# One chunk in one of eight widths for the last 512 rows of the second feed-forward, with a short last block packed

## The chip, the cores and the metric

The kernel runs on one core of one Trainium2 chip. The metric is the device time of one execution in microseconds. Each kernel is timed in several runs, and the median is quoted. The profile is of one further execution.

## The reference

Three stages follow one another, on float32 data (the last stage's weights come as float64).

```python
x = attention(q, k, v)                     # 1536 rows of 512
logits = x @ w_gate                        # 8 experts
expert_idx = np.argmax(logits, axis=1)
for i in range(N):                         # capacity 384 rows for each expert
    e = expert_idx[i]
    if counts[e] < capacity:
        disp[e, counts[e]] = x[i]; counts[e] += 1; keep[i] = True
y = relu(disp @ w1) @ w2                   # for each expert
out[i] = gate_w[i] * y[...] if keep[i] else 0
h = out @ w_in                             # 512 -> 2048
g = relu(h) ** 2
return g @ w_out                           # 2048 -> 512
```

A row that its expert has no room for is zero after the second stage, and so is its row of the result: relu of zero, squared, times `w_out`. The inputs are drawn from one fixed seed. The reference's own routing of them fills the experts with 290, 123, 98, 163, 117, 165, 92 and 488 rows; clipped at 384 each, 1432 rows are kept.

## The kernel before

The expert stage writes its results to a DRAM buffer `yd`, with expert after expert packed without gaps (`off` holds where each starts, `dst` each row's place, L787 to L793). Kept rows are therefore rows 0 to 1431 of `yd`; the rest stay as they were filled, with zeros and a token number that is out of bounds. Each row of `yd` carries its token's number in a last column.

The second feed-forward (L1022 to L1105) works in that packed order. Its 1536 rows are cut into four chunks, 512, 512, 256 and 256 (`chunks`, L949). A chunk has 16 steps `f`, one for each 128 of the 2048 hidden units. All products are made of float32 numbers split into a high and a low part of fp32r, three products (high by high, high by low, low by high) for each:

- `stage_a` (L1038, matmuls L1049): 12 matmuls, 4 parts of the depth by 3 products, each with the chunk's rows as moving columns (512 or 256), into the tile `a`; then ScalarE's relu into `xb` (L1051) and VectorE's square (L1052).
- `stage_g` (L1055): ScalarE rounds the squares to the high part `gh` (L1060), VectorE subtracts for the low part `gl` (L1061).
- `stage_b` (L1064, matmuls L1073): for each block `t` of 128 rows, 3 matmuls with 128 rows of `gh` or `gl` as weights and 512 columns of `w_out` moving. They add up in PSUM over the 16 steps, in one tile `out` for each block. After step 15, `out` is copied to a `raw` tile, by VectorE for even `t` (L1080) and ScalarE for odd `t` (L1078), and GpSimd issues an indirect DMA that scatters the 128 rows to their tokens (L1081). Rows whose token number is out of bounds are not written.

The order of work is written out by hand: `stage_a` of step i, `stage_g` of step i, `stage_b` of step i-1. TensorE runs this order without reordering. A scatter is declared free of a conflict with the one issued just before it, not with the one two before; so each scatter waits until the second last has landed.

The rows of the next chunk are loaded and transposed during the chunk before (`load_y`, L951; transposes L968, four for each block of 128 rows), at steps 7, 9, 11 and 13.

Run-time branches exist already. Ahead of the expert stage every engine reads the eight counts and `head` (the row at which the last expert starts) from the tile `cnt` into registers (L989, L991, written by VectorE at L788 to L790). `more` (L926) runs a further block of 128 rows for an expert only if its count asks for it, and L1018 loads the first chunk again if `head` is below 512.

Of the kernel before, what the change touches and what calls it, by code (L numbers as in the profile page):

```python
# [8 lines left out]
F32 = mybir.dt.float32  # L9
F32R = mybir.dt.float32r  # L10
BF16 = mybir.dt.bfloat16
I32 = mybir.dt.int32
# [4 lines left out]
P = 128  # L17
# [16 lines left out]
def kernel(  # L34
# [15 lines left out]
    nc = tc.nc  # L50
    B, H, S, D = q.shape
    NTOK, DM = out.shape
    E = w_gate.shape[1]
# [5 lines left out]
    NFF = FF // P  # L59
# [6 lines left out]
    nblk = (cap + P - 1) // P  # L66
# [10 lines left out]
    const = ctx.enter_context(tc.tile_pool(name="const", bufs=1))  # L77
# [7 lines left out]
    banks = dict(s=[0, 1], pt=[2], ot=[3], bg=[4, 5, 6], lg=[7])  # L85

    def ps(tag, name):
        banks[tag].append(banks[tag].pop(0))
        return psum.tile([P, 512], F32, tag=f"b{banks[tag][-1]}", name=name)
# [7 lines left out]
    stream, held, eager, slot = [], 0, False, 0  # L97
# [193 lines left out]
    tok = const.tile([P, NQB], I32, name="tok")  # L291
# [29 lines left out]
    if fast:  # L321
# [22 lines left out]
        for g in range(3 if stack else 1):  # L344
            x = own[g * HS : (g + 1) * HS]
            nc.gpsimd.affine_select(x, x, pattern=[[-NS, H], [0, D]], compare_op=ALU.is_ge, fill=0.0, base=0, channel_multiplier=1)
            nc.gpsimd.affine_select(x, x, pattern=[[NS, H], [0, D]], compare_op=ALU.is_ge, fill=0.0, base=NS - 1, channel_multiplier=-1)
    else:
        for j in range(NJ):
            m = ap_.tile([P, S], F32, name=f"m{j}")  # L350
# [366 lines left out]
    for u in range(len(units) + PL + 1):  # L717
# [4 lines left out]
        if u < len(units):  # L722
            n, c = units[u]
# [17 lines left out]
        m, c = divmod(u, HP)  # L741
# [30 lines left out]
    if nblk:  # L772
        src = xrp.tile([P, nblk, E], I32, name="src")
        nc.vector.tensor_scalar(src.rearrange("p b e -> p (b e)"), inv, float(NOBODY), None, op0=ALU.add)
        free = const.tile([P, nblk, E], F32, name="free")
        nc.vector.tensor_scalar(
            free.rearrange("p b e -> p (b e)"), inv, 0.0, float(NOBODY), op0=ALU.is_ge, op1=ALU.mult
        )
        p_ = ps("lg", "cnt")
        nc.tensor.matmul(p_[:, :E], ones, runoh, start=True, stop=True)  # L780
        cntf = const.tile([P, E], F32, name="cntf")
        nc.vector.tensor_scalar(cntf, p_[:, :E], float(cap), None, op0=ALU.min)

        off = const.tile([P, E], F32, name="off")
        nc.vector.memset(off[:, 0:1], 0.0)
        for e in range(1, E):
            nc.vector.tensor_add(off[:, e : e + 1], off[:, e - 1 : e], cntf[:, e - 1 : e])  # L787
        cnt = const.tile([P, E + 1], I32, name="cnt")  # L788
        nc.vector.tensor_copy(cnt[:, :E], cntf)
        nc.vector.tensor_copy(cnt[:, E:], off[:, E - 1 :])  # L790
        dst = const.tile([P, nblk, E], I32, name="dst")
        nc.vector.tensor_add(free, free, spot.unsqueeze(2).to_broadcast([P, nblk, E]))
        nc.vector.tensor_add(dst, free, off.unsqueeze(1).to_broadcast([P, nblk, E]))  # L793
    att.__exit__(None, None, None)
    banks = dict(s=[0, 1, 2], iv=[3], pt=[4], ot=[5], bg=[6, 7])
# [15 lines left out]
    def x_at(e, b):  # L811
        return xring[min(b, XB - 1), e % 2]

    def gate_at(e, b):
        return gate[2 + b % 2 if b else e % 2]
# [9 lines left out]
    def pre(e, b):  # L825
        if e >= E or b >= nblk:
            return
        p_ = ps("bg", "xT")
        for c in range(KD):
            nc.tensor.transpose(p_[:, c * P : (c + 1) * P], x_at(e, b)[:, c * P : (c + 1) * P], ident)  # L830
        xT[e, b] = xTs[min(b, 1)]
        h_, l_ = (x.rearrange("p c n -> p (c n)") for x in xT[e, b])
        nc.scalar.copy(h_, p_)
        nc.vector.tensor_sub(l_, p_, h_.bitcast(F32))
        g_ = gate_at(e, b)
        nc.vector.tensor_scalar(g_, x_at(e, b)[:, DM:], 1e-9, None, op0=ALU.add)
        nc.vector.reciprocal(g_, g_)
# [108 lines left out]


    CH = 512
    chunks = [(c0, CH) for c0 in range(0, NTOK - CH, CH)] + [(NTOK - CH, CH // 2), (NTOK - CH // 2, CH // 2)]  # L949
    NCH = len(chunks)  # L950
    x2T = {0: tuple(x2p.tile([P, KD, CH], F32R, name="x2A" + x) for x in "hl")}  # L951
    last = (E - 1) % 2
# [2 lines left out]
    def load_y(c, tags):  # L955

        c0, w = chunks[c]

        def ld(t):
            if t < w // P:  # L960
                r0 = c0 + t * P
                nc.sync.dma_start(yts[t % len(yts)], yd[r0 : r0 + P, :])

        def go(t):
            yt = yts[t % len(yts)]
            p_ = ps(tags[t % 2], "x2T")
            for kk in range(KD):
                nc.tensor.transpose(p_[:, kk * P : (kk + 1) * P], yt[:, kk * P : (kk + 1) * P], ident)  # L968
            n = c0 // P + t
            nc.gpsimd.tensor_copy(tok[:, n : n + 1], yt.bitcast(I32)[:, DM:])  # L970
            pv = p_.rearrange("p (k n) -> p k n", k=KD)
            hv, lv = (x[:, :, t * P : (t + 1) * P] for x in x2T[c])
            nc.scalar.copy(hv, pv)
            nc.vector.tensor_sub(lv, pv, hv.bitcast(F32))
            ld(t + len(yts))

        for t in range(len(yts)):
            ld(t)
        return [lambda t=t: go(t) for t in range(w // P)]
# [9 lines left out]
        vals = [nc.values_load(cnt[0:1, e : e + 1], min_val=0, max_val=cap) for e in range(E)]  # L989
    if nblk:  # L990
        head = nc.values_load(cnt[0:1, E : E + 1], min_val=0, max_val=NTOK)  # L991
    pre(0, 0)
    its = []
    for e in range(E):
        g = e + 1
# [28 lines left out]
    ffp = ctx.enter_context(tc.tile_pool(name="ffp", bufs=1, side="right"))  # L1024
    WO.alloc()
    x2T[1] = tuple(ffp.tile([P, KD, CH], F32R, name="x2B" + x) for x in "hl")
    for c in range(2, NCH - 1):
        x2T[c] = x2T[c % 2]
    x2T[NCH - 1] = tuple(x[:, :, CH // 2 :] for x in x2T[NCH - 2])
    zf = zb.bitcast(F32)  # L1030
    zw = zf.shape[1]
    for t in range(NQB):
# [3 lines left out]
    outp, gT, its, scattered = {}, {}, [], []  # L1036

    def stage_a(c, f):  # L1038
        nonlocal its
        if f == 0:  # L1040
            its = load_y(c + 1, ("pt", "ot")) if c + 1 < NCH else []
        a_ = ps("bg", "a")
        xh, xl = x2T[c]
        w = chunks[c][1]
        for kk in range(KD):
            r = slice(f % 2 * 512 + kk * P, f % 2 * 512 + kk * P + P)
            wh, wl = WI.h[f // 2][:, r], WI.l[f // 2][:, r]
            for m, (a, bb) in enumerate(((wh, xh), (wh, xl), (wl, xh))):
                nc.tensor.matmul(a_[:, :w], a, bb[:, kk, :w], start=(kk == 0 and m == 0), stop=(kk == KD - 1 and m == 2))  # L1049
        r_ = xring[f % 2, last][:, :w]  # L1050
        nc.scalar.activation(r_, a_[:, :w], AF.Relu)  # L1051
        nc.vector.tensor_mul(r_, r_, r_)  # L1052
        gT[c, f] = r_

    def stage_g(c, f):  # L1055
        r_ = gT[c, f]
        gh = ffp.tile([P, CH], F32R, tag="gh", name="gh", bufs=2)
        gl = ffp.tile([P, CH], F32R, tag="gl", name="gl", bufs=2)
        gh, gl = (x[:, : chunks[c][1]] for x in (gh, gl))
        nc.scalar.copy(gh, r_)  # L1060
        nc.vector.tensor_sub(gl, r_, gh.bitcast(F32))  # L1061
        gT[c, f] = (gh, gl)

    def stage_b(c, f):  # L1064
        gh, gl = gT.pop((c, f))
        if f == 0:
            outp[c] = [ps("s" if t < 3 else "iv", "out") for t in range(chunks[c][1] // P)]
        wh, wl = WO.h[f // 2], WO.l[f // 2]
        r = slice((f % 2) * 512, (f % 2) * 512 + 512)
        for t in range(chunks[c][1] // P):  # L1070
            cs = slice(t * P, (t + 1) * P)
            for m, (a, bb) in enumerate(((gh, wh), (gh, wl), (gl, wh))):
                nc.tensor.matmul(outp[c][t], a[:, cs], bb[:, r], start=(f == 0 and m == 0), stop=(f == NFF - 1 and m == 2))  # L1073
            if f == NFF - 1:
                n = chunks[c][0] // P + t
                o_ = raw_tile()[:, :DM]
                if t % 2:
                    nc.scalar.copy(o_, outp[c][t])  # L1078
                else:
                    nc.vector.tensor_copy(o_, outp[c][t])  # L1080
                i = nc.gpsimd.indirect_dma_start(  # L1081
                    out=out, out_offset=bass.IndirectOffsetOnAxis(ap=tok[:, n : n + 1], axis=0), in_=o_, in_offset=None,
                    bounds_check=NTOK - 1, oob_is_err=False,
                )

                if scattered:
                    tc.declare_no_dep(i.ins, scattered[-1].ins, reason="rows of different tokens")
                scattered.append(i)

    steps = [(c, f) for c in range(NCH) for f in range(NFF)]  # L1090
    def tick():
        if not ticks.done():
            ticks.tick()

    for i in range(len(steps) + 1):
        if i < len(steps):
            c, f = steps[i]
            turn = f >= 7 and f % 2 and its
            stage_a(c, f)
            tick()  # L1100
            stage_g(c, f)
            if turn:
                its.pop(0)()
        if i >= 1:
            stage_b(*steps[i - 1])  # L1105


# [27 lines left out]
```

## Time and profile before

| | us |
|---|---|
| median of 3 runs | 624.29 |
| lowest and highest of them | 622.31, 625.81 |
| the profiled execution's own time | 622.56 |
| span of the profiled execution | 620.8 |
| first matmul of the second feed-forward, from the span's start | 333.15 |
| its third chunk (rows 1024 to 1279) begins on TensorE | 518.60 |
| its last `stage_b` begins on TensorE | 611.14 |
| last scatter is issued | 614.89 |

Times in the rows count from the span's start. The profiled execution's own time is 1.76 us above its span. PE is TensorE's matmul unit, PEld its weight load, DVE VectorE, ACT ScalarE, POOL GpSimd, SP the queue that issues plain DMAs; a `q` behind a name is that engine's sequencer, which runs ahead of the engine. Matmuls are pipelined: the duration of one row overlaps the next matmul's, so rates are read from start to start.

### The profile page before, as it was taken

Reading aid. Unit: us, or ns where it says so; the run is one execution under the profiler, and the core shown is the slowest. Engines: PE = TensorE matmul, PEld = TensorE weight load, DVE = VectorE, ACT = ScalarE, POOL = GpSimd, SP = SyncE. Lnnn points to the kernel's source line nnn. Section 1 sums busy time; section 2 is a strip of 40 time slices with the busy share of each in tenths; the row PEclk is TensorE's granted clock in tenths of the full one; section 3 lists DMA queues with packets and bytes.
Section 4 is the critical chain, followed back from the end, with each engine's and each line's share of the span. In section 5 each row is a group of like instructions: output and inputs, shape, how many; then the busy total and the mean of one; then the engine's idle time right before and its main releaser. Section 6 shows DMA issues by size and latency. Waiting matters only on the chain. (4 is left out here: it accounts for less than half of the span.)

```text
span 620.8 us, 9781 instructions
## 1 busy us (share of the span) xinstructions
PE 588.8 (95%) x3437; PEld 470.4 (76%) x3439; DVE 359.6 (58%) x847; ACT 305.1 (49%) x681; POOL 136.3 (22%) x235
## 2 busy tenths in 40 slices
PE   7999999979999999998798999999999999999994
PEld 4778777738887777776676777888888888998983
DVE  3788888647259967948544899983222323333331
ACT  4888878626247847646423456553212222323221
POOL 8444544342134413431010000000200001101001
PEclk9999999979999999999899899999999999999998
DMA  8697994456337966857482555610100000000000
GB/s 183 160 224 153 236 184 127 141 141 205 126 108 269 341 205 200 314 172 248 142 304 70 190 167 202 199 39 0 69 1 17 18 0 35 35 1 35 1 1 20
DMA packets 74664, 81.99 MB, mean 132 GB/s; under 512 B 42248, under 2 KB 53512, under 8 KB 74608
## 3 DMA queue, kind: packets, MB, share of 16 engines
q1 hardware_dynamic: 70608, 72.45, 40.3%
q0 software_dynamic: 4000, 8.82, 4.1%
q8 instruction: 32, 0.52, 0.3%
q14 instruction: 24, 0.20, 0.1%
HBM read 69.29 MB, written 16.27 MB: 138 GB/s over the span
## 5 line engine op out<-in xcount | busy, mean ns | idle before, releaser
L1051 ACT ACTIVATE xb<-a 128x512 f32<-128x512 f32 (+1 forms) x64 | 31.5, 492 | 151.6 <-PE a L1049 151.6
L1052 DVE TENSOR_TENSOR xb<-xb 128x512 f32<-128x512 f32 (+1 forms) x64 | 35.8, 559 | 116.8 <-ACT xb L1051 116.8
L1073 PE MATMUL out<-yh,gl 128*128 128x512 f32 x192 | 76.8, 400 | 2.4 <-DVE gl L1061 2.1
L1073 PE MATMUL out<-yh,gh 128*128 128x512 f32 x192 | 77.4, 403 | 0.5 <-ACT gh L1060 0.5
L1073 PE MATMUL out<-yl,gh 128*128 128x512 f32 x192 | 76.5, 399 | 0.0
L1049 PE MATMUL a<-x2Ah,xh 128*128 128x256 f32 (+1 forms) x192 | 61.5, 320 | 0.3 <-PEq L1018 0.3
L1049 PE MATMUL a<-x2Al,xh 128*128 128x256 f32 (+1 forms) x192 | 61.3, 320 | 0.2 <-DVEq L1018 0.2
L1049 PE MATMUL a<-x2Ah,xl 128*128 128x256 f32 (+1 forms) x192 | 61.1, 318 | 0.0
L1081 POOL DMA_INDIRECT out_dram<-raw,tok x12 | 12.0, 998 | 215.4 <-DVE raw L1080 168.9
L451 ACT ACTIVATE p<-p,nm 128x260 f32<-128x260 f32 (+2 forms) x96 | 46.8, 489 | 17.1 <-DVE nm L439 16.0
L1061 DVE TENSOR_TENSOR gl<-xb,gh 128x512 fp32r<-128x512 f32 (+1 forms) x64 | 35.6, 557 | 27.5 <-PE out L1073 14.4
L916 POOL DMA_INDIRECT yd<-ys,dst x14 | 25.5, 1819 | 116.2 <-POOLq L926 50.5
L1060 ACT CAST gh<-xb 128x512 fp32r<-128x512 f32 (+1 forms) x64 | 32.9, 514 | 29.4 <-DVE xb L1052 29.4
L1073 PEld LDWEIGHTS out<-yh,gl 128*128 128x128 f32 x192 | 36.5, 190 | 13.4 <-DVE gl L1061 4.4
L146 DVE TENSOR_TENSOR yl<-raw,yh 128x512 fp32r<-128x512 f32 x64 | 40.4, 685 | 6.2 <-ACT yh L145 6.2
L1073 PEld LDWEIGHTS out<-yh,gh 128*128 128x128 f32 x192 | 36.3, 189 | 7.9 <-ACT gh L1060 1.4
L1073 PEld LDWEIGHTS out<-yl,gh 128*128 128x128 f32 x192 | 36.5, 190 | 7.2
L1049 PEld LDWEIGHTS a<-x2Ah,xh 128*128 128x128 f32 x192 | 36.1, 188 | 5.0 <-issue 0.7
L1049 PEld LDWEIGHTS a<-x2Al,xh 128*128 128x128 f32 x192 | 36.1, 188 | 4.7 <-DVEq L1018 0.5
L1049 PEld LDWEIGHTS a<-x2Ah,xl 128*128 128x128 f32 x192 | 36.4, 189 | 2.9
L145 ACT CAST xh<-raw 128x512 fp32r<-128x512 f32 x64 | 36.3, 619 | 1.2 <-DMA raw<-in_moe_w_dram 0.9
L145 ACT CAST yh<-raw 128x512 fp32r<-128x512 f32 x64 | 35.5, 624 | 2.6 <-PEq L926 1.7
(199 smaller groups left out, 1398.6 us busy)
## 6 DMA issues: line engine op xcount, KB each, us to landing
raw<-in_moe_w_dram SPq DMA_DIRECT2D x64, 512.0 KB, 5.0
raw<-in_moe_w_in_dram SPq DMA_DIRECT2D x16, 512.0 KB, 4.9
raw<-in_moe_w_out_dram SPq DMA_DIRECT2D x8, 1024.0 KB, 4.8
yd<-zero SPq DMA_DIRECT2D x12, 256.5 KB, 5.8
xd<-x SPq DMA_DIRECT2D x12, 256.5 KB, 5.4
xb<-yd SPq DMA_DIRECT2D x12, 256.5 KB, 3.2
kr<-in_k_dram SPq DMA_DIRECT2D x12, 256.0 KB, 6.1
qr<-in_q_dram SPq DMA_DIRECT2D x12, 256.0 KB, 7.0
```

Of the source, the lines that this page charges most:

```text
L145: (hi or nc.scalar.copy)(self.h[i][:, sl], t[:, sl])
L146: (eng or nc.vector).tensor_sub(self.l[i][:, sl], t[:, sl], self.h[i].bitcast(F32)[:, sl])
L451: nc.scalar.activation(d["p"][:, h, :width], d["p"][:, h, :width], AF.Exp, bias=d["nm"][:, h : h + 1], scale=-1.0, accum_out=d["sm"][:, h ...
L916: nc.gpsimd.indirect_dma_start(out=yd[:, :], out_offset=bass.IndirectOffsetOnAxis(ap=dst[:, b, e : e + 1], axis=0), in_=y_, in_offset=None ...
L1049: nc.tensor.matmul(a_[:, :w], a, bb[:, kk, :w], start=(kk == 0 and m == 0), stop=(kk == KD - 1 and m == 2))
L1051: nc.scalar.activation(r_, a_[:, :w], AF.Relu)
L1052: nc.vector.tensor_mul(r_, r_, r_)
L1060: nc.scalar.copy(gh, r_)
L1061: nc.vector.tensor_sub(gl, r_, gh.bitcast(F32))
L1073: nc.tensor.matmul(outp[c][t], a[:, cs], bb[:, r], start=(f == 0 and m == 0), stop=(f == NFF - 1 and m == 2))
L1081: i = nc.gpsimd.indirect_dma_start(out=out, out_offset=bass.IndirectOffsetOnAxis(ap=tok[:, n : n + 1], axis=0), in_=o_, in_offset=None, bo ...
```

## The change

The last two chunks of 256 rows become one chunk of 512 rows of storage. How many of them are computed is chosen at run time. A ninth value is read into registers, `total`, the number of kept rows (VectorE adds the last expert's start and its count). After step 0 of `stage_a` and `stage_g` of that chunk, and the last `stage_b` of the chunk before, every engine compares and branches through a tree of three levels to one of eight copies of the remaining code, for 0, 128, 256, 320, 384, 416, 448 or 512 rows: the least that is not below `total` - 1024. In such a copy `stage_a` has `w` moving columns, and `stage_b` has the blocks that `w` needs.

If `w` leaves a last block of 64 rows or fewer (32 for 416, 64 for 448 and 320), that block is packed: the low parts of its `k_` rows stand behind their high parts in the tile `gh`, in columns `w` to `w + k_`, so that one weight load of `2 k_` columns has both. Two matmuls then take the place of three (high and low together by the weights' high part, and by their low part). The packed block's `out` has the high rows' sums in its first `k_` partitions and the low rows' in the next; at the end ScalarE copies the second group to `raw`, VectorE adds the first. The packed block goes first in `stage_b`.

```diff
-        cnt = const.tile([P, E + 1], I32, name="cnt")
+        cnt = const.tile([P, E + 2], I32, name="cnt")
...
+        nc.vector.tensor_add(cnt[:, E + 1 :], off[:, E - 1 :], cntf[:, E - 1 :])
...
-    chunks = [(c0, CH) for c0 in range(0, NTOK - CH, CH)] + [(NTOK - CH, CH // 2), (NTOK - CH // 2, CH // 2)]
+    chunks = [(c0, CH) for c0 in range(0, NTOK, CH)]
...
+        total = nc.values_load(cnt[0:1, E + 1 :], min_val=0, max_val=NTOK)
...
+    def packed(c):
+        return width[c] % P if 0 < width[c] % P <= 64 else 0
+
     def stage_g(c, f):
...
+        w, k_ = width[c], packed(c)
+        gh, gl = ghl[f % 2]
+        nc.scalar.copy(gh[:, :w], r_)
+        if w > k_:
+            nc.vector.tensor_sub(gl[:, : w - k_], r_[:, : w - k_], gh.bitcast(F32)[:, : w - k_])
+        if k_:
+            nc.vector.tensor_sub(gh[:, w : w + k_], r_[:, w - k_ :], gh.bitcast(F32)[:, w - k_ : w])
...
     def stage_b(c, f):
...
+        ts = list(range(nt))
+        if k_:
+            ts = ts[-1:] + ts[:-1]
+        for t in ts:
...
+            if k_ and t == nt - 1:
+                prods = ((gh[:, cs.start : w + k_], wh), (gh[:, cs.start : w + k_], wl))
+                o = o[: 2 * k_, :]
+            else:
+                prods = ((gh[:, cs], wh), (gh[:, cs], wl), (gl[:, cs], wh))
+                o = o[:rows, :]
...
+                if k_ and t == nt - 1:
+                    nc.scalar.copy(o_[:k_, :], o[k_ :, :])
+                    nc.vector.tensor_add(o_[:k_, :], o_[:k_, :], o[:k_, :])
...
+                scatter(n, o_, rows)
...
+    full = NFF * (NCH - 1) + 1 if nblk else len(steps)
+    prev = run(steps[:full], None)
+
+    def rest(ws):
+
+        if len(ws) > 1:
+            mid = len(ws) // 2
+            with tc.If(total > chunks[-1][0] + ws[mid - 1]) as cmp:
+                rest(ws[mid:])
+            with cmp.Else():
+                rest(ws[:mid])
+            return
...
+        if k_:
+            nc.vector.tensor_copy(gh[:, w : w + k_], gl.bitcast(F32)[:, w - k_ : w])
+        if w:
+            stage_b(*run(steps[full:], prev))
...
+    if nblk:
+        rest([0, 128, 256, 320, 384, 416, 448, 512])
+    else:
+        stage_b(*prev)
```

The code for 416 rows is reached by one taken branch: the first comparison (above 1344) holds and goes on into the code that follows, the second (above 1472) does not and jumps, the third (above 1408) holds. TensorE's instructions at the place where the jump lands, in the changed kernel (`a` is the tile of `stage_a`, `x2A` are parts of `w_in`, `xh` and `xl` the rows, `yh` and `yl` parts of `w_out`; some 730 matmuls for 512 and 448 rows stand between the first comparison and this one):

```order
L1147 UNCONDITIONAL_BRANCH
L1147 COMPARE_AND_BRANCH
L1050 MATMUL a<-x2Ah,xh_4936 128x416
...
L1106 MATMUL out<-yh_5302,gh_5332 64x512 [waits DVE_49,Activation_49]
L1106 MATMUL out<-yl_5303,gh_5332 64x512
L1106 MATMUL out<-yh_5302,gh_5332 128x512
L1106 MATMUL out<-yl_5303,gh_5332 128x512
L1106 MATMUL out<-yh_5302,gl_5333 128x512
```

No branch of this tree has a wait of its own. The packed block's two matmuls stand ahead of the three blocks of three.

GpSimd's last instructions before the change (`out_dram` is the result, `tok` the token numbers; the bracket holds what the instruction waits for, `DMASW6` and its like being one earlier scatter each):

```order
L970 COPY tok<-xb_197 128x1 [waits DMAHW2_49]
L970 COPY tok<-xb_201 128x1 [waits DMAHW3_49]
L1081 DMA out_dram<-raw_75,tok 1536x512 [waits DMASW6_49,DVE_49,Pool_49]
L1081 DMA out_dram<-raw_75,tok 1536x512 [waits DMASW7_49,Activation_49,Pool_49]
L1081 DMA out_dram<-raw_76,tok 1536x512 [waits DMASW0_49,DVE_49,Pool_49]
L1081 DMA out_dram<-raw_76,tok 1536x512 [waits DMASW1_49,Activation_49,Pool_49]
```

And in the code for 416 rows of the changed kernel:

```order
L1147 COMPARE_AND_BRANCH
L1075 DMA out_dram<-raw_75,tok 1536x512 [waits DMASW6_49,DVE_49,Pool_49]
L1075 DMA out_dram<-raw_75,tok 1536x512 [waits DMASW7_49,DVE_49]
L1075 DMA out_dram<-raw_76,tok 1536x512 [waits DMASW0_49,Activation_49]
L1075 DMA out_dram<-raw_76,tok 1536x512 [waits DMASW1_49,DVE_49]
L1147 UNCONDITIONAL_BRANCH
```

The four waits on earlier scatters are the same. Before, the first two of these scatters belong to the third chunk and the last two to the fourth, 16 steps later; now all four come after the last step of one chunk, the third waiting for the first to land and the fourth for the second.

## Rows read from the trace of the kernel before

**Rows 1.** The page: busy time of the engines, and the instruction DMA queue (packets, MB).

```profile
PE 588.8 (95%) x3437; PEld 470.4 (76%) x3439; DVE 359.6 (58%) x847; ACT 305.1 (49%) x681; POOL 136.3 (22%) x235
...
q8 instruction: 32, 0.52, 0.3%
```

**Rows 2.** The chain that ended last, 512 us on: start, us, engine, tile and line.

```profile
512.99 2.81 PE a L1049 x12
...
518.60 1.42 PE a L1049 x12
520.02 2.80 PE out L1073 x12
522.82 1.42 PE a L1049 x12
524.24 1.40 PE out L1073 x6
...
541.17 0.44 PE x2T L968 x4
...
611.14 1.67 PE out L1073 x6
```

**Rows 3.** Busy us by stretch; last three columns granted clock, DMA share, GB/s.

```profile
614.00:616.00 2.00, 0.00 (x0) 0.00 (x0) 0.00 (x0) 0.00 (x0) 1.56 (x2) 1.00 0.34 131
616.00:618.00 2.00, 0.00 (x0) 0.00 (x0) 0.00 (x0) 0.00 (x0) 0.00 (x0) 0.54 0.08 25
```

**Rows 4.** TensorE's waits: us in total, times, longest; then one line's instructions, 188 to 202 us.

```profile
PE h L858 <- PEq L926: 1.0, 3, 0.4
...
L926 PEldq COMPARE_BRANCH  x1: 3598/3598/3598, 199.9 to 199.9; - x1
```

**Rows 5.** Timeline of TensorE around that comparison.

```profile
203.08 0.40 PE L884 MATMUL y<-xh,hTl 128*128 128x512 f32 x1
203.66 0.47 PE L858 MATMUL h<-yh,xT0h 128*128 128x512 f32 x1 [0.18 <-PEq L926]
```

**Rows 6.** Reads of the value `head` into TensorE's register, ns.

```profile
L991 PEldq TENSOR_LOAD <-cnt x1: 308/308/308, 135.7 to 135.7; - x1
```

**Rows 7.** Timeline of all engines, last step of `stage_b`.

```profile
611.14 0.50 PE L1073 MATMUL out<-yh,gh 128*128 128x512 f32 x1
...
611.48 0.39 PE L1073 MATMUL out<-yl,gh 128*128 128x512 f32 x1
...
612.14 0.69 DVE L1080 COPY raw<-out 128x512 f32<-128x512 f32 x1 [0.59 <-PE out L1073]
...
612.84 0.59 ACT L1078 COPY raw<-out 128x512 f32<-128x512 f32 x1 [1.75 <-PE out L1073]
```

**Rows 8.** Timeline of GpSimd: the scatters of the second chunk and the last chunk.

```profile
523.24 0.99 POOL L1081 DMA_INDIRECT out_dram<-raw,tok  x1 [81.09 <-DVE raw L1080]
524.53 0.98 POOL L1081 DMA_INDIRECT out_dram<-raw,tok  x1 [0.30 <-issue]
527.35 0.98 POOL L1081 DMA_INDIRECT out_dram<-raw,tok  x1 [1.84 <-DMA out_dram<-raw,tok]
528.63 1.13 POOL L1081 DMA_INDIRECT out_dram<-raw,tok  x1 [0.30 <-issue]
...
613.60 0.98 POOL L1081 DMA_INDIRECT out_dram<-raw,tok  x1 [40.68 <-ACT raw L1078]
614.89 0.98 POOL L1081 DMA_INDIRECT out_dram<-raw,tok  x1 [0.30 <-issue]
```

**Rows 9.** Timeline of TensorE after its longest wait in the second feed-forward.

```profile
342.80 0.55 PE L1073 MATMUL out<-yh,gl 128*128 128x512 f32 x1 [2.11 <-DVE gl L1061]
343.15 0.63 PE L1073 MATMUL out<-yh,gh 128*128 128x512 f32 x1
343.58 0.63 PE L1073 MATMUL out<-yl,gh 128*128 128x512 f32 x1
```

**Rows 10.** That stretch by windows, columns as in rows 3.

```profile
343.00:345.00 2.00, 2.00 (x6) 1.55 (x6) 2.00 (x3) 1.92 (x3) 0.00 (x0) 0.53 0.79 273
```

More of the change, by code (lines that the diff above doesn't have):

```diff
@@ L787 @@
             nc.vector.tensor_add(off[:, e : e + 1], off[:, e - 1 : e], cntf[:, e - 1 : e])
-        cnt = const.tile([P, E + 1], I32, name="cnt")
+        cnt = const.tile([P, E + 2], I32, name="cnt")
         nc.vector.tensor_copy(cnt[:, :E], cntf)
-        nc.vector.tensor_copy(cnt[:, E:], off[:, E - 1 :])
+        nc.vector.tensor_copy(cnt[:, E : E + 1], off[:, E - 1 :])
+        nc.vector.tensor_add(cnt[:, E + 1 :], off[:, E - 1 :], cntf[:, E - 1 :])
         dst = const.tile([P, nblk, E], I32, name="dst")
@@ L1026 @@
     x2T[1] = tuple(ffp.tile([P, KD, CH], F32R, name="x2B" + x) for x in "hl")
-    for c in range(2, NCH - 1):
+    for c in range(2, NCH):
         x2T[c] = x2T[c % 2]
-    x2T[NCH - 1] = tuple(x[:, :, CH // 2 :] for x in x2T[NCH - 2])
     zf = zb.bitcast(F32)
@@ L1043, in stage_a @@
         xh, xl = x2T[c]
-        w = chunks[c][1]
+        w = width[c]
         for kk in range(KD):
@@ L1053, in stage_a @@
         gT[c, f] = r_
+    ghl = [tuple(ffp.tile([P, CH], F32R, name=f"g{x}{i}") for x in "hl") for i in range(2)]
+    def packed(c):
+        return width[c] % P if 0 < width[c] % P <= 64 else 0
     def stage_g(c, f):
         r_ = gT[c, f]
[L1057 to L1061, printed above, removed]
@@ L1062, in stage_g, with scatter @@
-        gT[c, f] = (gh, gl)
+        w, k_ = width[c], packed(c)
[5 more added lines that the diff above has]
+            nc.vector.tensor_sub(gh[:, w : w + k_], r_[:, w - k_ :], gh.bitcast(F32)[:, w - k_ : w])
+        gT[c, f] = (gh, gl)
+    def scatter(n, o_, rows):
+        i = nc.gpsimd.indirect_dma_start(
+            out=out, out_offset=bass.IndirectOffsetOnAxis(ap=tok[:rows, n : n + 1], axis=0), in_=o_[:rows, :], in_offset=None,
+            bounds_check=NTOK - 1, oob_is_err=False,
+        )
+        if scattered:
+            tc.declare_no_dep(i.ins, scattered[-1].ins, reason="rows of different tokens")
+        scattered.append(i)
@@ L1064, in stage_b @@
     def stage_b(c, f):
         gh, gl = gT.pop((c, f))
+        w, k_ = width[c], packed(c)
+        nt = (w + P - 1) // P
         if f == 0:
-            outp[c] = [ps("s" if t < 3 else "iv", "out") for t in range(chunks[c][1] // P)]
+            outp[c] = [ps("s" if t < 3 else "iv", "out") for t in range(nt)]
         wh, wl = WO.h[f // 2], WO.l[f // 2]
         r = slice((f % 2) * 512, (f % 2) * 512 + 512)
[L1070 to L1073, printed above, removed]
+        ts = list(range(nt))
@@ new lines, in stage_b @@
+        if k_:
+            ts = ts[-1:] + ts[:-1]
+        for t in ts:
+            cs = slice(t * P, min(w, (t + 1) * P))
+            rows = cs.stop - cs.start
+            o = outp[c][t]
+            if k_ and t == nt - 1:
[4 more added lines that the diff above has]
+                o = o[:rows, :]
+            for m, (a, bb) in enumerate(prods):
+                nc.tensor.matmul(o, a, bb[:, r], start=(f == 0 and m == 0), stop=(f == NFF - 1 and m == len(prods) - 1))
@@ L1076, in stage_b @@
                 o_ = raw_tile()[:, :DM]
-                if t % 2:
-                    nc.scalar.copy(o_, outp[c][t])
-                else:
[L1080 to L1090, printed above, removed]
+                if k_ and t == nt - 1:
+                    nc.scalar.copy(o_[:k_, :], o[k_ :, :])
+                    nc.vector.tensor_add(o_[:k_, :], o_[:k_, :], o[:k_, :])
+                elif t % 2:
+                    nc.scalar.copy(o_[:rows, :], o)
+                else:
+                    nc.vector.tensor_copy(o_[:rows, :], o)
+                scatter(n, o_, rows)
     def tick():
@@ L1093, in tick, with run @@
             ticks.tick()
-    for i in range(len(steps) + 1):
-        if i < len(steps):
-            c, f = steps[i]
+    def run(steps, prev):
+        for c, f in steps:
             turn = f >= 7 and f % 2 and its
@@ L1103 @@
                 its.pop(0)()
-        if i >= 1:
-            stage_b(*steps[i - 1])
+            if prev:
+                stage_b(*prev)
+            prev = c, f
+        return prev
+    width = [CH] * NCH
+    steps = [(c, f) for c in range(NCH) for f in range(NFF)]
+    full = NFF * (NCH - 1) + 1 if nblk else len(steps)
[8 more added lines that the diff above has]
+            return
+        nonlocal banks, outp, gT, scattered, slot
+        kept = {k: list(v) for k, v in banks.items()}, dict(outp), dict(gT), list(scattered), slot
+        w = width[-1] = ws[0]
+        k_ = packed(NCH - 1)
+        gh, gl = gT[prev]
+        if k_:
+            nc.vector.tensor_copy(gh[:, w : w + k_], gl.bitcast(F32)[:, w - k_ : w])
+        if w:
+            stage_b(*run(steps[full:], prev))
+        banks, outp, gT, scattered, slot = kept
+    if nblk:
+        rest([0, 128, 256, 320, 384, 416, 448, 512])
+    else:
+        stage_b(*prev)
 _INS = ["q", "k", "v", "moe_w_gate", "moe_w1", "moe_w2", "moe2_w_in", "moe2_w_out"]
```

## The prediction

> **What bounds the kernel now.** I read the page's busy times first: TensorE's matmuls fill 588.8 of 620.8 us, and no other engine is above 76% [rows 1]. A share is only an average, so the second view is the chain that ended last, over the stretch that the change rewrites [rows 2]. The reader is to see there that it is TensorE alone: each row begins where the one above ends, `a` and `out` in turn, and the times are set by the work. A step of 512 rows takes 2.81 us for `a` and 2.80 us for `out`; one of 256 rows takes 1.42 and 1.40 us. Four transposes for one block of rows take 0.44 us. So in this stretch a matmul that is left out is time saved, and the question is what the end and the jump cost.
>
> The third view decides which of the eight copies runs. Each kept row is a row of 2048 bytes that a scatter writes. The fourth chunk's two scatters moved (131 + 25) GB/s x 2 us = 312 KB, which is 152 rows, not 256 [rows 3]. So 1280 + 152 = 1432 rows are kept, as the reference's routing has it. The last 512 rows hold 408 of them: the copy for 416, with a packed block of 32.
>
> **TensorE's work.** Before, from 518.60 to the start of the last `stage_b` at 611.14 are 92.54 us [rows 2]. The parts add up: 32 x 1.42 + 2.80 + 31 x 1.40 + 2 x 0.44 = 92.5.
>
> Now:
> - Step 0 of `a` is still made for 512 rows, 2.81 us, and the second chunk's last `out` takes 2.80 us as before.
> - Fifteen `a` of 416 columns. Between the two measured widths the line gives 1.42 + (2.81 - 1.42) x 160/256 = 2.29 us.
> - Fifteen `out` ahead of the last. Eleven matmuls of 512 columns instead of twelve: 2.80 x 11/12 = 2.57 us. I price the matmuls with 64 weight columns like the others, since the moving columns are the same; no row here shows this form.
> - 2.81 + 2.80 + 15 x (2.29 + 2.57) = 78.5 us.
> - The transposes of two blocks move into the second chunk, so it ends 2 x 0.44 = 0.88 us later [rows 2].
>
> The last `stage_b` starts 92.54 - 78.5 - 0.88 = 13.2 us earlier. The pipeline ahead of it (relu, square, high, low) is longer for 416 columns than for 256, but so is the `out` that hides it, and the packed part adds one small subtraction; I change nothing there and allow 0.3 us to either side. In the steps before, each square has a whole `a` and a whole `out` as cover, 4.9 us, so the added VectorE instruction costs nothing. If it were late, the packed block would wait first.
>
> **The jump.** The first bound is nothing: TensorE's sequencer runs ahead of the engine. The nearest rows are the branches of the expert stage. Three times TensorE waited on them, 1.0 us in all and 0.4 us at most [rows 4]. At 203.08 and 203.66 two matmuls start 0.58 us apart, where 2.81/12 = 0.23 is usual, so that one cost 0.35 us [rows 5]. The comparison ahead of it held the sequencer for 3.6 us, from 199.9 on [rows 4], so some 3 us were hidden. I take 0.4 us; the upper end is 3.6 us with no cover. The comparisons are free of waits, but they stand behind earlier instructions of their engine; ScalarE and VectorE have the 2.3 us of the next `a` as cover, and after that the `out` of a step whose squares are made already, all but a copy of 32 columns.
>
> **The added register.** One more read costs TensorE's sequencer 0.31 us [rows 6], just ahead of the expert stage's first transposes, and VectorE's extra addition stands ahead of all the reads. Bounds 0 and 0.5 us; I take 0.3 us.
>
> **The end.** This is where I expect a third of the gain to go. Count from the start S of the last `stage_b`. Before, S is 611.14; VectorE's copy starts at S + 1.00, after three products, and ends at 612.83; the first scatter is issued 0.77 us later, at S + 2.46, the second 1.29 us behind it, and the span ends 5.9 us after that, at S + 9.7 [rows 7, 8].
>
> Now four scatters have to leave. The second chunk shows how four behave: the third is issued 4.11 us after the first, having waited for it to land, and the fourth 4.10 us after the second [rows 8]. Step by step:
> - The packed block has two products, the second starting 0.34 us after the first and lasting 0.39 us: S + 0.77 with 0.04 us to the reader [rows 7].
> - ScalarE's copy, 0.59 us, VectorE's addition, 0.69 us (both priced as the copies of 128 rows, since the columns are the same) and 0.03 us between: S + 2.08. Then 0.77 us as before: the first scatter at S + 2.85.
> - The second at S + 4.14. The third waits for the first, to S + 6.96.
> - The fourth waits for the second, to S + 4.14 + 4.10 = S + 8.24. Every other block is copied by S + 4, so copies are not what it waits for.
> - The span ends 5.9 us after it: S + 14.15 against S + 9.66.
>
> That costs 4.5 us. If a scatter of 32 rows lands sooner, the third comes sooner, but the fourth still waits for the second, which has 128 rows. The low end is a queue paced by its issue alone: the fourth at 2.85 + 3 x 1.29, a cost of 3.0 us. The unconditional branches at a copy's end lie beside these 11 us.
>
> **Sum.** -13.2 + 0.4 + 0.3 + 4.5 = -8.0 us. Against the profiled execution, 622.56 us (1.76 above its span), that is 614.6; against the median of the three runs, 624.29, it is 616.3. The four executions scatter by 3.5 us, and the middle of the inner two, 623.4, is my base: 615.4 us.
>
> **Rival 1: the jump is not hidden.** Some 730 matmuls are jumped over, where the expert stage's branches skip two bodies of about 53. TensorE's 6876 instructions came in 32 packets [rows 1], so this target is several packets on and cannot be there yet if they come one by one. Price: 3.6 us instead of 0.4. A wait that long has another cost. After TensorE had stood for 2.11 us, matmuls started 0.43 us apart instead of 0.23, eight of them [rows 9], and the granted clock of that stretch was 0.53, that is near the lower of its two levels, 1.2 GHz [rows 10]. Eight times 0.20 is 1.6 us. Together +4.8 us: 620.2. For it speaks the distance; against it the 3 us by which the sequencer runs ahead. The Trainium skill (Runtime: NRT & Kernel Launch, section on instruction fetch mechanics) speaks against the change here: a taken branch to code outside the prefetched window waits for a fetch by DMA. By that rule 620.2 would be the time; the trace agrees only in the one long comparison, whose cost TensorE hardly saw. Chance 0.12.
>
> **Rival 2: it does not do what it says, since a wide copy runs.** Were more than 1472 rows kept, the copy for 512 would run: 15 x (2.81 + 2.80) + 5.61 + 0.88 = 90.6 us, a gain of 1.9, with nothing for a jump; the end costs 4.1 (the first scatter at S + 2.46, the last at S + 7.86). Net +2.5 us: 625.9, no change by measure. Rows 3 speak against it. Chance 0.02.
>
> **Rival 3, slower: the code behind the jump comes late again and again.** The copy has 356 matmuls and as many weight loads; at 6876/32 = 215 instructions for a packet that is four packets. If nothing is fetched ahead after a jump and each holds TensorE as in rival 1, 4 x (3.6 + 1.6) = 20.8 us are lost: 635.8. It decides once the waits together pass the 8.0 us gained, and counts as slower from 11. Against it: straight code in rows 2 has no such holes, at the same pace. Chance 0.02.
>
> **How the numbers follow.** The forecast, between 613 and 617.5, has 0.82. Some 0.02 stay for what I have not thought of. The low end of the range is the sum with the cheap ends (no jump, no register, 3.0 for the end), -10.2, from the lower base: 612.5. The high end takes a jump of 3.6 us at full clock and the median as base: 619.5. A measurement of this kernel can tell about 0.5%, 3.1 us, from no change: faster means under 620.3. Rival 1 sits on that line and is halved. Faster 0.90, within 0.5% 0.08, slower 0.02.
>
> **What would show it.** Right: `a` in a row of 12 taking near 2.29 us and `out` x11 near 2.57; no wait of TensorE above 0.6 us between the second chunk and the third; a last `stage_b` some 12.5 us earlier than 611.14; and at the end four scatters, the last waiting for a landing and issued near S + 8.2. Wrong: `a` taking 2.8 us at 416 columns; a wait of several us behind the branch, with clock 0.5 after it; four scatters 1.29 us apart; another copy than the one for 416.

## The result and the profile after

The changed kernel takes 614.86 us (median of 4 runs) against 624.54 us (median of 4) for the kernel before: a ratio of 0.9857, 95% interval 0.9828 to 0.9885. One of its four executions, at a granted clock of 0.556, took 925.95 us; it counts in that median but not in the ratio, and the other three took 613.72 to 615.59 us. The forecast was 615.4 us.

| us | before | after | difference |
|---|---|---|---|
| the profiled execution's own time | 622.56 | 615.59 | -6.97 |
| its span | 620.8 | 613.9 | -6.9 |
| expert stage and all before it, to the first matmul of the second feed-forward | 333.15 | 335.21 | +2.06 |
| from there to the third chunk's first `a` | 185.45 | 186.07 | +0.62 |
| from there to the last `stage_b` | 92.54 | 78.07 | -14.47 |
| from there to the span's end | 9.66 | 14.55 | +4.89 |

The last four lines add up to the difference of the spans. Each can be read in the rows. First the chain that ended last, from the third chunk on (start, us, engine, tile and line), which answers to [rows 2]:

```profile
521.28 2.81 PE a L1050 x12
524.09 2.80 PE out L1106 x12
526.89 2.24 PE a L1050 x12
529.13 2.57 PE out L1106 x11
...
594.44 2.26 PE a L1050 x12
596.70 2.56 PE out L1106 x11
599.27 0.09 issue
599.35 0.66 PE out L1106 x2
```

`a` of 416 columns takes 2.24 to 2.26 us and `out` with eleven matmuls 2.57 us; the copy for 416 rows ran, as it has rows of 12 and 11. TensorE goes from the second chunk into this copy without a gap. The next rows are the matmuls on both sides of the jump, and then TensorE's comparisons there (ns least, median, most; first and last start):

```profile
526.50 0.39 PE L1106 MATMUL out<-yh,gl 128*128 128x512 f32 x1
526.72 0.35 PE L1050 MATMUL a<-x2Ah,xh 128*128 128x416 f32 x1
```

```profile
L1147 PEldq COMPARE_BRANCH  x3: 68/73/3618, 522.5 to 526.4; - x3
```

The matmuls start 0.22 us apart, the usual distance, although the taken comparison held the sequencer for 3.6 us. It began at 522.7, some 4 us before the engine had run out of work. This answers to [rows 4, 5]. Between 522.5 and 526.1 us the trace has one DMA packet, on the instruction queue q8 (packets, MB, share of 16 engines' time):

```profile
q8 instruction: 1, 0.02, 2.0%
```

In the 27 us ahead of it no packet of any queue moved.

The end, GpSimd's scatters, answers to the last rows of [rows 8]:

```profile
602.13 0.89 POOL L1075 DMA_INDIRECT out_dram<-raw,tok  x1 [68.00 <-DVE raw L1116]
603.32 0.99 POOL L1075 DMA_INDIRECT out_dram<-raw,tok  x1 [0.30 <-issue]
606.60 0.98 POOL L1075 DMA_INDIRECT out_dram<-raw,tok  x1 [2.30 <-DMA out_dram<-raw,tok]
607.89 0.99 POOL L1075 DMA_INDIRECT out_dram<-raw,tok  x1 [0.30 <-issue]
```

With S at 599.35 the four are issued at S + 2.78, 3.97, 7.25 and 8.54. The third waits 2.30 us for a landing. The row of the fourth names no landing: it follows the third at the distance that issuing alone takes. The span ends 6.0 us after the last.

The 2.06 us ahead of the second feed-forward lie where no code of the chunk runs. The timeline of TensorE at the start of the expert stage shows them, the first row from the kernel before, the others after:

```profile
136.27 0.66 PE L830 MATMUL xT<-ident,xb 128*128 128x128 f32 x4 [0.19 <-DMA xb<-xd,src]
...
136.95 0.66 PE L831 MATMUL xT<-ident,xb 128*128 128x128 f32 x4 [1.92 <-DMA xb<-xd,src]
138.40 0.50 PE L859 MATMUL h<-xh,xT0h 128*128 128x512 f32 x1 [0.80 <-ACT xT0h L834]
...
140.17 0.63 PE L859 MATMUL h<-xh,xT0l 128*128 128x512 f32 x1
140.60 0.63 PE L859 MATMUL h<-xh,xT0h 128*128 128x512 f32 x1
```

The gathered rows came 0.7 us later than in the trace of before. TensorE stood for 1.92 us, and then matmuls started 0.43 us apart, in a stretch with a granted clock of 0.52, near the lower level of 1.2 GHz:

```profile
139.50:143.00 3.50, 3.50 (x10) 2.73 (x9) 1.62 (x3) 0.41 (x1) 2.59 (x3) 0.52 0.56 150
```

(In a row of this view the last three columns are granted clock, DMA share and GB/s.) Whether the added register read causes this was open; two runs below answer it.

### The profile page after: what moved, and what is told of

It is laid out like the page before. It is cut to its first block, busy times and chain, and to the rows that moved or that the text cites. A ratio compares the mean times of both kernels' runs of the same rounds, so it can differ in the third digit from the quotient of the medians.

```text
span 613.9 us, 9330 instructions
## 1 busy us (share of the span) xinstructions
PE 577.7 (94%) x3231; PEld 457.4 (75%) x3231; DVE 353.2 (58%) x833; ACT 296.2 (48%) x649; POOL 135.8 (22%) x235
## 5 line engine op out<-in xcount | busy, mean ns | idle before, releaser
L1106 PE MATMUL out<-yh,gh 128*128 128x512 f32 (+1 forms) x192 | 77.1, 401 | 0.6 <-ACT gh L1067 0.5
L1106 PE MATMUL out<-yl,gh 128*128 128x512 f32 (+1 forms) x192 | 76.6, 399 | 0.0
L1050 PE MATMUL a<-x2Ah,xh 128*128 128x512 f32 (+1 forms) x128 | 48.1, 376 | 0.3 <-PEq L1020 0.3
L1050 PE MATMUL a<-x2Al,xh 128*128 128x512 f32 (+1 forms) x128 | 47.9, 374 | 0.2 <-DVEq L1020 0.2
L1050 PE MATMUL a<-x2Ah,xl 128*128 128x512 f32 (+1 forms) x128 | 47.8, 374 | 0.0
L1106 PEld LDWEIGHTS out<-yh,gh 128*128 128x128 f32 (+1 forms) x192 | 35.6, 185 | 9.6 <-ACT gh L1067 0.9
L1106 PEld LDWEIGHTS out<-yl,gh 128*128 128x128 f32 (+1 forms) x192 | 35.5, 185 | 8.4
L874 DVE TENSOR_TENSOR hTl<-hT,hTh 128x512 fp32r<-128x512 f32 x28 | 19.3, 690 | 28.1 <-ACT hTh L873 25.5
L146 DVE TENSOR_TENSOR xl<-raw,xh 128x512 fp32r<-128x512 f32 x48 | 30.1, 687 | 1.9 <-ACT xh L145 1.8
L526 PE MATMUL ot<-pts,v 128*64 128x128 f32 x352 | 30.1, 286 | 0.5 <-ACT pts L493 0.5
```

The costliest lines, as they stand in the source:

```text
L146: (eng or nc.vector).tensor_sub(self.l[i][:, sl], t[:, sl], self.h[i].bitcast(F32)[:, sl])
L526: nc.tensor.matmul(d["o"][i * D : (i + 1) * D, c * P : (c + 1) * P], vt[b, kb][:, h, :], t_, start=i not in d["started"], stop=False, skip ...
L1106: nc.tensor.matmul(o, a, bb[:, r], start=(f == 0 and m == 0), stop=(f == NFF - 1 and m == len(prods) - 1))
```

## The experiments

Seven kernels in two sets; those of one set ran on one chip. The ratios are to the kernel before, which ran beside each set (621.92 us in the first, 622.95 us in the second, medians of 17 runs).

**The changed kernel again.** No edit beyond an empty line.

> The changed kernel once more, beside the other kernels of this set. Both theories: about 0.986 of the kernel before, some 614 to 615 us. It also tells whether the late start of the expert stage seen after the change (first expert matmul at 138.40 us instead of 137.72, then eight or nine matmuls at the clock's lower level) belongs to the added register read. If it does, this run shows both again; if it is scatter between executions, it may show neither.

Measured: 613.1 us, ratio 0.9867 (0.9843 to 0.9891). Its first expert transposes begin at 136.69 us after a wait of 1.30 us, its first expert matmul at 138.14, and no matmul behind it is at the lower clock; the second feed-forward begins at 333.06 us. So the register is read here too, without the late start. S is at 595.92, the span ends at 610.0, S + 14.08.

**No branches, no register.** The code for 416 rows stands alone.

```diff
-        nc.vector.tensor_add(cnt[:, E + 1 :], off[:, E - 1 :], cntf[:, E - 1 :])
...
-        total = nc.values_load(cnt[0:1, E + 1 :], min_val=0, max_val=NTOK)
...
-        rest([0, 128, 256, 320, 384, 416, 448, 512])
+        rest([416])
```

> The tree of branches, the ninth register and VectorE's addition are taken out; the code for 416 rows stands alone. Theory (TensorE's sequencer runs ahead, so the jump is hidden): the same time as the changed kernel, faster by 0 to 0.5 us, and the matmuls between the second and the third chunk start 0.23 us apart in both. Rival (jump and register cost what I summed or more): 0.7 us faster or more; and if the late start of the expert stage comes from the register read, 2 us faster, with the first expert matmul back near 137.7 us.

Measured: 612.37 us, ratio 0.9859 (0.9829 to 0.989), against 0.9867 in the same set: 0.5 us, within the intervals. The chain shows the same passage into the third chunk:

```profile
519.45 2.81 PE a L1048 x12
522.26 2.80 PE out L1104 x12
525.06 2.25 PE a L1048 x12
527.31 2.57 PE out L1104 x11
...
597.53 0.66 PE out L1104 x2
```

And without the register the expert stage begins no earlier (TensorE's timeline):

```profile
137.05 0.66 PE L830 MATMUL xT<-ident,xb 128*128 128x128 f32 x4 [0.99 <-DMA xb<-xd,src]
```

From the third chunk's start (519.45) to the last `stage_b` (597.53) are 78.08 us, against 78.07 and 78.09 in the two traces with the tree: the jump costs TensorE nothing. The register's 0.3 us is less than these times can tell from nothing. The late start after the change was scatter of one execution: here the gathered rows come later still, and the second feed-forward begins at 333.15 us.

**Two far jumps.** The tree becomes a row of comparisons, widest first.

```diff
-            mid = len(ws) // 2
+            mid = len(ws) - 1
```

> The tree becomes a row of comparisons, widest first: the code for 416 rows is reached by two taken branches, each over some 360 matmuls, one right behind the other. Theory (a far jump holds the sequencer for 3.6 us and only its lead over the engine hides it): the first jump uses the lead up, the second is seen in full, TensorE waits 3 us or more behind the second chunk, the clock falls after it, and the kernel is 3 to 5 us slower than the changed one. Rival (a far jump costs little, and the long comparison was the sequencer waiting for room in TensorE's queue): TensorE waits under 0.5 us and the time is that of the changed kernel.

Measured: 619.98 us, ratio 0.9956 (0.9931 to 0.9981), slower than the changed kernel in the same set by 6.9 us by the medians and 5.5 us by the ratios, where 3 to 5 us were expected. The chain around the jumps, and TensorE's comparisons there:

```profile
520.71 2.81 PE a L1050 x12
523.52 2.80 PE out L1106 x12
526.32 4.31 issue
530.63 4.52 PE a L1050 x12
535.15 2.69 PE out L1106 x11
537.85 2.25 PE a L1050 x12
...
605.49 0.66 PE out L1106 x2
```

```profile
L1147 PEldq COMPARE_BRANCH  x3: 70/3581/4829, 522.0 to 530.5; - x3
```

Two of the three comparisons, the taken ones, held the sequencer for 3.6 and 4.8 us, 8.4 us together from 522.0 on. TensorE had work until 526.3 and then stood for 4.31 us. What followed ran at half speed: `a` of 416 columns took 4.52 us instead of 2.26, and the windows have the clock at its lower level until then:

```profile
530.00:533.00 3.00, 2.37 (x7) 2.30 (x8) 0.00 (x0) 0.00 (x0) 1.18 (x2) 0.50 0.25 94
533.00:535.00 2.00, 2.00 (x8) 1.82 (x7) 0.00 (x0) 0.00 (x0) 0.78 (x1) 0.50 0.67 260
535.00:538.00 3.00, 3.00 (x14) 2.37 (x13) 1.25 (x3) 1.06 (x2) 0.00 (x0) 0.95 0.01 1
```

4.3 us of waiting, 2.26 us in `a` and 0.1 us in the first matmuls of `out` make 6.7 us. So does the chunk: from its first `a` at 520.71 to the last `stage_b` at 605.49 are 84.8 us, against 78.1. The two profiles' spans differ by more, 9.8 us; 2.9 us of that lie ahead of the third chunk, where both kernels run the same work. Three of the twelve executions took only 615.5 to 616.4 us, with a granted clock of 0.984 over the execution, against 0.976 to 0.981 in the other nine; no trace of them is kept, so what they were spared stays open.

The theory stands; its size was too small because the second hold was longer than 3.6 us and the clock took 2.4 us. The rival, that the long comparison is only a sequencer waiting for room in TensorE's queue, falls: TensorE stood idle for 4.31 us with the sequencer held. What goes with a hold can be read from the instruction queue q8, here from 522.0 to 525.6 us and from 525.6 to 530.6 us:

```profile
q8 instruction: 1, 0.02, 2.0%
...
q8 instruction: 2, 0.03, 4.5%
```

In the six traces with a tree these jumps make seven holds, of 3.3 to 4.8 us, and in each a packet of this queue starts 0.7 to 1.0 us after the hold does. Without branches none starts between 522.5 and 550 us. That the hold is a wait for this packet is not shown beyond this coincidence in time. A far jump is not cheap. It was hidden.

**Scatters freed of each other.** They write rows of different tokens.

```diff
-        if scattered:
-            tc.declare_no_dep(i.ins, scattered[-1].ins, reason="rows of different tokens")
+        for x in scattered:
+            tc.declare_no_dep(i.ins, x.ins, reason="rows of different tokens")
```

> Each scatter is declared free of a conflict with all scatters before it, not with the last one alone, so that the third of the last four does not wait for the first to land. They write rows of different tokens. Theory (the end is paced by these waits): the four scatters are issued 1.3 us apart, the last near S + 6.7 instead of S + 8.5, and the kernel is 1.9 us faster than the changed one. Rival (the end is paced by something else, the queue's own work or the landings themselves): the last scatter lands no earlier, 0 to 0.5 us gained.

Measured: 611.99 us, ratio 0.9842 (0.9818 to 0.9865), against 0.9867 in the same set. GpSimd's last scatters:

```profile
601.15 0.89 POOL L1075 DMA_INDIRECT out_dram<-raw,tok  x1 [69.02 <-issue]
602.35 0.99 POOL L1075 DMA_INDIRECT out_dram<-raw,tok  x1 [0.30 <-issue]
603.64 0.99 POOL L1075 DMA_INDIRECT out_dram<-raw,tok  x1 [0.30 <-issue]
604.94 0.98 POOL L1075 DMA_INDIRECT out_dram<-raw,tok  x1 [0.30 <-issue]
```

No wait for a landing is left. With S at 598.38 the last is issued at S + 6.56 and the span ends at S + 12.5, 1.6 us sooner than in the run of the changed kernel beside it and 2.0 us sooner than in its first profile. The trace shows the mechanism; the two ratios differ by 1.6 us as well, but their intervals overlap.

**No packing.**

```diff
-        return width[c] % P if 0 < width[c] % P <= 64 else 0
+        return 0
```

> The changed kernel without the packing: the last block of 32 rows has three products and a low part of its own, and stands last. Theory (a matmul costs its 512 moving columns, however few weight columns it has): one matmul more in each of 16 steps, 16 x 0.234 = 3.7 us on TensorE; the end is 0.4 us shorter, since the first scatter no longer waits for a copy and an addition; 3.3 us slower than the changed kernel. Rival (the packing's second copy, addition and subtractions cost about what it saves): within 1 us of the changed kernel.

Measured: 618.89 us, ratio 0.9939 (0.9916 to 0.9962). The chain has twelve matmuls again in each `out`:

```profile
525.49 2.25 PE a L1050 x12
527.74 2.81 PE out L1106 x12
530.54 2.26 PE a L1050 x12
```

From the first narrow `a` at 525.49 to the last `stage_b` at 601.31 are 75.8 us, against 72.5 (526.89 to 599.35) with packing: 3.4 us, near the 3.7 expected. The end was 14.1 us from S, not shorter than in the run of the changed kernel (14.08): the first scatter left 0.4 us earlier, but the third came 4.1 us after it, and the fourth 4.5 us after the second. By the ratios of the two sets packing is worth 4.5 us, with some 2 us of uncertainty; the trace accounts for 3.4 of them. That packing gives back what it saves is excluded.

**Full width.** One chunk of 512 rows, nothing narrowed.

```diff
-        rest([0, 128, 256, 320, 384, 416, 448, 512])
+        rest([512])
```

> One chunk of 512 rows in full width, no branches, the register kept: only the joining of the two last chunks is left. Theory (the narrower width is the whole gain, and the four scatters at the end cost 4 us): 2.5 us slower than the kernel before, 11 to 12 us slower than the changed one. Rival (joining the chunks is itself the gain, as fewer steps with longer matmuls): faster than the kernel before.

Measured: 624.9 us, ratio 1.0023 (1.0006 to 1.004), 1.4 us slower than before. The chain, and from TensorE's timeline the first matmul of the last `stage_b`:

```profile
519.61 2.81 PE a L1050 x12
...
525.22 2.79 PE a L1050 x12
```

```profile
609.15 0.40 PE L1106 MATMUL out<-yh,gh 128*128 128x512 f32 x1
```

From the third chunk's second `a` at 525.22 to the last `stage_b` at 609.15 are 83.9 us, the 84.2 of rival 2. The span ends at S + 13.35. From the chunk's start at 519.61 it is 89.5 us, and 0.9 us of transposes lie before it: joining the two chunks alone gains 2.1 us on TensorE and costs 3.7 us at the end; all of the gain is in the width and the packing. The width alone is the difference from the run without packing, which ran beside it: 0.9939 against 1.0023, 5 us. Against the changed kernel 11 to 12 us were expected; by the ratios of the two sets it is 9.7. Against the kernel before the size was 1.1 us off, 0.4 of it at the end, where the third scatter came 3.5 us after the first instead of 4.1.

**Freed scatters, packed block last.** The edit of the freed scatters (called e3 in the expectation), and

```diff
-        if k_:
-            ts = ts[-1:] + ts[:-1]
```

> The scatters are freed as in e3, and the packed block goes last in each step, not first. Theory: the first scatter leaves after three products and one copy, at S + 2.5 instead of S + 2.8, and the last step no longer begins with the block whose packed parts come last; the four scatters still follow 1.3 us apart, or the packed block's copy and addition set the last one, near S + 6.4; 0.3 us faster than e3. Rival: no difference from e3, or slower, if the packed block's copy and addition come too late at the end.

Measured: 611.32 us, ratio 0.9815 (0.9795 to 0.9834). This is faster than the kernel before, and than the changed kernel as it ran again (0.9867 in the other set, whose interval lies above); from the changed kernel's first ratio (0.9857) and from the freed scatters alone (0.9842) the intervals do not part it. GpSimd's last scatters:

```profile
600.03 0.98 POOL L1075 DMA_INDIRECT out_dram<-raw,tok  x1 [68.26 <-ACT raw L1112]
...
603.89 0.89 POOL L1075 DMA_INDIRECT out_dram<-raw,tok  x1 [0.31 <-issue]
```

With S at 597.67 the first leaves at S + 2.36, the last at S + 6.22, and the span ends at S + 12.1, 0.4 us sooner than with the freed scatters alone. The last step also begins without the 0.25 us that TensorE waits when the packed block, whose parts are ready last, comes first (597.90 to 598.38 with the freed scatters alone, 597.44 to 597.67 here, where 0.23 is usual).

## Why the prediction was right

- **What bounds the kernel.** TensorE alone, in this stretch: this held. What was taken from it brought the last `stage_b` forward by as much; the end gave part of it back.
- **Which copy.** The 152 rows read from [rows 3] gave the copy for 416, and it ran.
- **TensorE's work.** Forecast 78.5 us from the third chunk's start to the last `stage_b`, measured 78.07. The line between 256 and 512 columns gave 2.29 us for `a`; it took 2.26. A matmul with 64 weight columns was priced like one with 128, and `out` took the forecast 2.57. The chunks before grew by 0.62 us, forecast 0.88. Here one pair of traces is not enough: the kernel without branches, whose clock fell after the early wait just as in [rows 10], grew by 0.85 us (186.30 against 185.45), and the changed kernel's second trace, in which it did not fall, is 0.7 us shorter than before (184.77).
- **The jump.** Forecast 0.4 us, measured none. The reason given, the sequencer's lead, is what the runs showed, and so is rival 1's mechanism. It did not decide because one jump of 3.6 us fits into a lead of 4 us, with some 0.4 us to spare. Two jumps gave the gap and the clock that rival 1 priced; its 1.6 us for the clock was too low, 2.4 us were lost. The Trainium skill (Runtime: NRT & Kernel Launch, section on instruction fetch mechanics) says that a taken branch outside the prefetched window waits for a fetch. The traces agree: every hold at these jumps, 3.3 to 4.8 us long, has a packet of the instruction queue q8 in it, and the code without branches has none there.
- **The register.** Forecast 0.3 us; not to be told from nothing. The second feed-forward starts at 333.15 us without the read and at 333.06 in the changed kernel's second trace, so no run here shows this term.
- **The end.** Forecast 4.5 us, measured 4.89 in the first profile and 4.4 in the second (14.08 against 9.66). The times hold one by one: the first scatter at S + 2.78 (forecast 2.85), the second at 3.97 (4.14), the third 4.47 us after the first (4.11) and the last at S + 8.54 (8.24). The reason given for the last does not: it was to wait for the second, but in both traces of the changed kernel it followed the third 1.29 us later and its row names no landing. In [rows 8] the fourth scatter of the second chunk already did the same. In these traces the third's wait sets the end; in the kernel without branches the fourth waited too, 0.77 us. That such waits pace the end was shown by taking them away.
- **The sum.** Forecast -8.0 us. The parts that belong to the change make -14.47 + 0.62 + 4.89 = -9.0 us in the first profile; 2.06 us of late start, of which none of the seven later traces has more than 1.3, hid some of it. TensorE's part, jump included, came to -13.85 instead of -12.8, the end to 4.89 instead of 4.5. The time came within 0.5 us of the forecast in part by luck: by the medians the gain was 9.7 us, 1.7 more than forecast, and the kernel before took 624.54 us, 1.1 more than the base.

## What to carry to other kernels

Where one engine's work is the time, leaving out a sixth of a stretch is worth that sixth, but four results that leave together at the end cost more than two: before two chunks are joined, walk the last step to the last transfer, one wait at a time. A far taken branch cost TensorE nothing while its sequencer was further ahead (4 us) than the branch held it (3.6 us), so a tree should put one such jump, and never two in a row, on the path that is taken. After a wait of TensorE, price the clock too: behind the two jumps the half-speed stretch cost another half of the wait.

## What was not expected

The time until a scatter has landed varies more than [rows 8] let one think: the third of the last four came 4.47, 4.06 and 2.97 us after the first, in the changed kernel's two profiles and in the one without branches. Kernels whose last transfers wait for each other carry this variation in their time.

A wait of 1.92 us ahead of the expert stage brought TensorE's lower clock in one execution (0.52 from 139.5 to 143 us); waits of 1.30, 0.99 and 1.45 us at the same place (the changed kernel again, without branches, with freed scatters) did not. The start of the first transposes does not tell them apart: 136.95 us with the fall, and 136.69, 137.05 and 136.97 us without.

Nor does a wait bring the same fall each time. All nine traces have a wait of 2.1 us early in the second feed-forward [rows 9], and in eight of them the granted clock then falls to near 0.5. In the changed kernel's second trace it does not:

```profile
342.72 0.50 PE L1107 MATMUL out<-yh,gl 128*128 128x512 f32 x1 [2.13 <-DVE gl L1070]
```

```profile
343.00:345.00 2.00, 2.00 (x10) 1.59 (x10) 2.00 (x4) 1.79 (x3) 0.31 (x1) 1.00 0.81 271
```

From the first matmul of the second feed-forward to the third chunk the nine traces take 184.8 to 187.5 us, for work that differs by 0.88 us at most. So two traces are compared stretch by stretch, with the clock of each beside it.
